# Masked pair products, and transposes and logits moved around one product, in a chunked delta-rule attention with expert routing

## The chip, the cores and the metric

The kernel runs on one core of one Trainium2 chip. The metric is the device time of one execution, in microseconds (us). A core has a matrix engine (TensorE, PE in the profile, with its weight loads listed as PEld), a vector engine (VectorE, DVE), an activation engine (ScalarE, ACT), a general engine (GpSimd, POOL) and a queue that issues transfers (SyncE, SP). Each engine runs its own instructions in order, and waits by semaphores for the others. Matrix products land in PSUM, eight banks of 2 KB per partition, from which ScalarE or VectorE copy them to SBUF.

## The reference

Two blocks follow each other. The first is the delta rule, for 4 batches, 8 heads, 768 steps and a head size of 48; the second sends each of the 3,072 resulting rows of 384 numbers through one of 16 experts, chosen by two argmax steps.

```python
k_n = k / (norm(k) + 1e-6)
for t in range(S):
    y[:, :, t] = q_t @ state
    v_old = state.T @ k_t
    state = state + beta_t * outer(k_t, v_t - v_old)
x = y as (B*S, H*D)
group = argmax(x @ w_group);  expert = argmax(x @ w_expert[group])
out = softmax weight of group * softmax weight of expert * (relu(x @ w1[expert]) @ w2[expert])
```

## The kernel before

**Tiling.** The 768 steps are cut into 24 chunks of 32 (`C = 32`, `NCH = 24`). The 4 batches of a chunk lie on the 128 partitions, 32 steps each (`quads`); `pairs` are the two halves of 64 partitions, two batches each. Four chunks make a group (`RG = 4`); a group's triangular systems, one per chunk, batch and head, are inverted together on VectorE with one system per partition.

**Stages.** `gram(u)` computes the products of keys with keys and of queries with keys of chunk u (L229). ScalarE copies the first to `gt` (L234), which the inverse reads, and, in `rest()`, the second to `raw` (L240); GpSimd multiplies `raw` with the triangular mask `upper` into `gq` (L242). Grams run nine chunks ahead (`LEAD = 9`). `inverse(g)` is VectorE's long task: a transpose of `gt` (L253), the norms, some 90 elimination steps (L304 to L332), and a transpose back into `mt` (L339). `spread(u)` has ScalarE copy `mt` twice into `mtb`, once for even and once for odd batches with zeros in the other (L347), so that one product of 64 rows and 64 columns can serve two batches.

`advance(u)` is the serial part, in five steps:
1. `a`: keys times the state, onto the scaled values in `a_ps` (L367, after VectorE's `scale`, L353); ScalarE copies it, negated, to `f` (L371); `o`: queries times the state into `o_ps` (L376)
2. `w` = inverse times `f` (L384), copied by ScalarE (L387)
3. the state product of keys and `w` into `s_ps` (L394), and ScalarE's copy of the first half of the state to `s_bd` (L401)
4. the copy of the second half
5. the inner outputs, `gq` times `w`, added to `o_ps` (L407), and the copy to `x` (L411)

`logits(u - 1)` has two steps for the chunk before: transposes of `x` (L428), copied to `xt` (L432), and the router's products (L436), copied to `lg` (L438). `route(r)` does the argmax, softmax, ranks (`rk`, L505) and places for a group of chunks on VectorE; its counts are products on TensorE (L499, L500); the sorting products (L540) gather each token's place into `s_sort`, a part of `s_ps`.

**PSUM.** `s_ps` holds four banks, `a_ps` and `o_ps` one each. `g_ps` is one tile of two banks, and is shared: Gram products use both, `w` bank 1, transposes and logits bank 0, the ranks' counts the end of bank 1.

**Order.** The order on each engine is written out by hand. The loop over u, from 0 to 24, calls the steps of `advance` and `logits` in turn, and between them `work(n)` and `allow(...)`. These feed the background tasks (`inverse`, `route`): `work(n)` gives each task n x 180 units times its share, and a task runs steps, each 100 units plus its elements, until its credit is spent. A task that yields a word (`NEXT`, `SOON`, `SORT`, `RANK`, `PE_STEP`, `ACT_STEP`, `TURN`) stands until `allow` is called with that word. `inverse(g)` for the group two ahead starts at the end of the period of the third chunk of a group, at share `SHARE`; the call of `gram` for its last chunk has just gone out. After the loop, the last routings are finished, the tokens' places are read, and the expert stage begins: 16 experts, two tiles of tokens each, nearly all on TensorE.

Of the kernel before, what the change touches and what calls it, by code (L numbers as in the profile page):

```python
# [8 lines left out]
F32 = mybir.dt.float32  # L9
# [5 lines left out]

C = 32
RG = 4
SHARE = 0.9
LEAD = 9
FIXED, TILE = 2, 128  # L20
SLOTS = [224] * FIXED + [232, 220, 214, 208, 204, 202, 200, 196, 192, 188, 184, 182, 176, 168]
# [4 lines left out]
def constants(n_tokens, seq, n_experts, n_group, n_batch):  # L26

    import numpy as np

    p = np.arange(128)  # L30
    i, k = np.meshgrid(np.arange(C), np.arange(C), indexing="ij")
    u = np.arange(n_tokens // 128)

    ids = np.stack([(p[:, None] // C) * seq + p[:, None] % C + u * C - n_tokens,
                    u * 128 + p[:, None]], axis=2)
    out = {
        "upper": np.concatenate([(i < k).astype(np.float32)] * n_batch, axis=0),
        "tiny": np.full((128, 1), 1e-36),
        "eps": np.full((128, 1), 1e-6),
        "parity": np.stack([p // C % 2 == b2 for b2 in range(2)], axis=1),  # L40
        "below": np.tile(-(i > k).astype(np.float32).reshape(1, C * C), (128, 1)),
        "ident": (p[:, None] == p[None, :]),
        "before": (p[:, None] < p[None, :]),
        "ones": np.ones((128, 128)),
        "desc": np.tile(np.arange(n_group, 0, -1), (128, RG)),
        "ids": ids.reshape(128, -1),

        "places": np.tile((2 * np.arange(TILE) + np.arange(2)[:, None]).reshape(1, -1), (128, 1)),


        "tie": np.tile(n_experts - 1 - np.arange(n_experts) + (1 << 20) * (np.arange(n_experts) < FIXED), (128, 1)),
        "slots": np.tile(SLOTS, (128, 1)),
        "expert": np.tile(np.arange(n_experts), (128, 1)),
    }
    at, n = {}, 0
    for name, a in out.items():
        at[name] = (n, n + a.shape[1])
        n += a.shape[1]
    return np.concatenate([a.astype(np.float32) for a in out.values()], axis=1), at
# [3 lines left out]
def deltanet_then_moe(  # L63
# [90 lines left out]
    with ExitStack() as first:  # L154
# [61 lines left out]
        def gram(u, home=None, parts=slice(0, 2)):  # L216


            g, uu = divmod(u, RG)
            kqt = kqt_[u % NB]  # L220
            if uu == 0 and parts.start == 0:
                gts[g] = wk.tile([128, C, RG, H], F32, tag="gt", name=f"gt{g}")
            g_out = (g_ps if home is None else home).rearrange("p f (j x) -> p (f j) x", j=NP)[:, :, 0:2 * C].rearrange(
                "p h (a t) -> p h a t", a=2)
            for j in range(NP):
                for b in range(B):
                    for hh in range(2):
                        rows = slice(hh * 64, hh * 64 + D)
                        nc.tensor.matmul(g_out[quads[b], hh * NP + j, parts],  # L229
                                         lhsT=kqt[rows, 0, j, quads[b]],  # L230
                                         rhs=kqt[rows, parts, j, quads[b]], start=True, stop=True,
                                         skip_group_check=True)
            if parts.start == 0:
                nc.scalar.activation(  # L234
                    gts[g][:, :, uu].rearrange("p t h -> p h t"), g_out[:, :, 0, :],
                    ACT.Copy)

            def rest():
                raw = wk.tile([128, H, C], F32, tag="raw", name=f"raw{u}")
                nc.scalar.activation(raw, g_out[:, :, 1, :], ACT.Copy)  # L240
                gqs[u] = wk.tile([128, H, C], F32, tag="gq", name=f"gq{u}", bufs=LEAD + 1)
                nc.gpsimd.tensor_tensor(  # L242
                    gqs[u], raw, cut["upper"][:, None, :].to_broadcast([128, H, C]), op=ALU.mult)

            return rest

        def inverse(g):

            m = wk.tile([128, C, C], F32, tag="m", name=f"m{g}")
            flat = m.rearrange("p i j -> p (i j)")
            nc.vector.transpose(out=flat, in_=gts.pop(g).rearrange("p t u h -> p (t u h)"))  # L253
# [105 lines left out]
        def advance(u):  # L359

            g, uu = divmod(u, RG)
            kqt = kqt_[u % NB]
            k = kv_[u % NV][:, 0:H * 64].rearrange("p (j d) -> p j d", j=NP)
            if u > 0:
                for j in range(NP):
                    for b in range(B):
                        nc.tensor.matmul(a_ps[quads[b], 2 * j:2 * j + 2, :],  # L367
                                         lhsT=kqt[:, 0, j, quads[b]], rhs=s_bd[:, b, j],
                                         start=False, stop=True, skip_group_check=True)
            f = wk.tile([128, H, D], F32, tag="f", name=f"f{u}")  # L370
            nc.scalar.activation(f, a_ps, ACT.Copy, scale=-1.0)  # L371
            o_ps = ps.tile([128, H, D], F32, tag="o", name=f"o_ps{u}")
            if u > 0:
                for j in range(NP):
                    for b in range(B):
                        nc.tensor.matmul(o_ps[quads[b], 2 * j:2 * j + 2, :],  # L376
                                         lhsT=kqt[:, 1, j, quads[b]], rhs=s_bd[:, b, j],
                                         start=(j == 0), stop=False, skip_group_check=True)
            yield
            mt = mtbs.pop(u)  # L380
            w_ps = g_ps[:, 1, 0:H * D].rearrange("p (h d) -> p h d", h=H)
            for h in range(H):
                for b in pairs:
                    nc.tensor.matmul(w_ps[b, h], lhsT=mt[b, (h % 2) * NP + h // 2],  # L384
                                     rhs=f[b, h], start=True, stop=True, skip_group_check=True)
            w = wk.tile([128, H, D], F32, tag="w", name=f"w{u}")
            nc.scalar.activation(w, w_ps, ACT.Copy)  # L387
            yield


            if u < NCH - 1:
                for j in range(NP):
                    for b in range(B):
                        nc.tensor.matmul(s_at[:, b, j], lhsT=k[quads[b], j],  # L394
                                         rhs=w[quads[b], 2 * j:2 * j + 2],
                                         start=(u == 0 and j == 0), stop=True,
                                         skip_group_check=True)
            for hh in range(2):
                rows = slice(hh * 64, hh * 64 + D)
                if u < NCH - 1:  # L400
                    nc.scalar.activation(s_bd[rows, :, :, hh, :],  # L401
                                         s_at[rows, :, :, hh * D:(hh + 1) * D], ACT.Copy)
                yield
            gq = gqs.pop(u)
            for h in range(H):
                for b in quads:
                    nc.tensor.matmul(o_ps[b, h], lhsT=gq[b, (h % 2) * NP + h // 2], rhs=w[b, h],  # L407
                                     start=(u == 0 and h == 0), stop=True,
                                     skip_group_check=True)
            x = wk.tile([128, DM], F32, tag="x", name=f"x{u}", bufs=4)  # L410
            nc.scalar.activation(x, o_ps.rearrange("p h d -> p (h d)"), ACT.Copy)  # L411
            xs[u] = x
            yield
# [134 lines left out]
        def start(task, share):  # L548
            behind.append(task)
            rate[task], due[task] = share, 0.0  # L550
# [33 lines left out]
        with tc.manual_schedule(engines={mybir.EngineType.PE, mybir.EngineType.DVE,  # L584
# [5 lines left out]
            masks = []  # L590
            for u in range(RG):
                gram(u, homes[u % len(homes)], slice(0, 1))
                if u == 0:
                    nc.tensor.matmul(a_ps.rearrange("p h d -> p (h d)"), lhsT=kqt_[0][:, 0, 0],
                                     rhs=kqt_[0][:, 0, 0:H * D // 128], start=True, stop=True)
                if u == 1:

                    nc.scalar.activation(kqt_[0][:, 1, 0, 0:1], cut["tiny"], ACT.Copy)
                    load_rest()
            start(inverse(0), 1)  # L600
            work(16)
            for i, u in enumerate(range(LEAD)):
# [18 lines left out]
            for u in range(NCH + 1):  # L621
# [12 lines left out]
                allow(ACT_STEP)  # L634
                if u + 1 < NCH and (u + 1) // RG in mts:
                    spread(u + 1)
                work(16)
                next(step)
                next(turned)
                allow(SORT)  # L640
                allow(RANK)
                if u and u + 1 < NCH:
                    scale(u + 1)
                work(9)
                next(step)
                next(turned)
                next(step)
                next(step)
                mask = gram(u + LEAD) if u + LEAD < NCH else lambda: None
                work(8)  # L650
                allow(PE_STEP)
                r = group_of.get(u - 1)
                if r is not None and group_of.get(u) != r and r >= NGR - 2:
# [281 lines left out]
```

## Time and profile before

The median of three runs is 571.86 us (570.44 to 572.13); the profiled execution has a span of 571.6 us.

| engine | busy us | share of the span | instructions |
|---|---|---|---|
| TensorE | 486.6 | 85% | 8376 |
| VectorE | 253.6 | 44% | 889 |
| ScalarE | 178.2 | 31% | 384 |
| GpSimd | 124.6 | 22% | 134 |

The shares mix two stages. The attention stage takes about the first 275 us, and VectorE's work lies nearly all in it; the expert stage takes the rest. A line of the timeline has a start, a duration, the engine, the line of the code, what it wrote and read, the shapes, a count of merged instructions, and in brackets the idle time before it with the instruction that ended it. The shape `64*64 64x48` on TensorE is 64 rows and 64 columns of weights, and 48 columns streamed.

### The profile page before, as it was taken

The numbers are of one execution on the slowest core, as the hardware profiler recorded it, in microseconds if no ns is written. First come the engines' busy times: TensorE is split into PE (matmuls) and PEld (weight loads), VectorE is DVE, ScalarE is ACT, GpSimd is POOL, SyncE is SP. The second block draws the span as 40 slices with busy tenths as digits, with TensorE's granted clock in tenths as the row PEclk, the third lists the DMA queues.
The fourth block names the chain that finished last, engine by engine and source line by source line (L and its number), as shares of the span: only waits on it lengthen the run. The fifth ranks groups of instructions, "written<-read, shape, count | busy, mean of one in ns | idle before, by whom it ended". The sixth has DMA issues, their size and how long they took to land.

```text
span 571.6 us, 18945 instructions
## 1 busy us (share of the span) xinstructions
PE 486.6 (85%) x8376; PEld 459.2 (80%) x8376; DVE 253.6 (44%) x889; ACT 178.2 (31%) x384; POOL 124.6 (22%) x134
## 2 busy tenths in 40 slices
PE   4227778788888887887699999999999999999993
PEld 3226667677787777787599999999999999999992
DVE  3999979799899597323601101011111111111110
ACT  2124436655664555651012111111111111111110
POOL 0130001121222111211432212342215321221111
PEclk9999768989986999997599999999999999999998
DMA  6913535766641123300157656676676775676400
GB/s 192 404 58 89 157 127 170 221 177 188 208 136 52 58 87 95 95 31 16 50 159 205 212 156 222 175 227 208 203 246 155 258 236 190 224 243 226 150 20 20
DMA packets 44900, 90.68 MB, mean 159 GB/s; under 512 B 9819, under 2 KB 29714, under 8 KB 44816
## 3 DMA queue, kind: packets, MB, share of 16 engines
q1 hardware_dynamic: 34832, 79.71, 42.6%
q0 software_dynamic: 9984, 9.74, 6.5%
q8 instruction: 67, 1.10, 0.8%
q14 instruction: 17, 0.14, 0.1%
HBM read 79.92 MB, written 9.66 MB: 157 GB/s over the span
## 4 chain that ended last, share of the span: by engine, by line
issue 33%; PE 21%; DVE 19%; POOL 12%; DMA 9%; ACT 4%; SPq 0%; POOLq 0%; ACTq 0%
DMA out_dram<-yo,to_i 8%; POOL xg L737 7%; POOL out_dram L788 5%; DVE t L326 4%; DVE m L332 4%; PE s_ps L394 3%; PE g_ps L384 3%; DVE m L309 3%; PE o_ps L407 2%; PE a_ps L367 2%; PE g_ps L229 2%; PE g_ps L436 2%; PE g_ps L428 2%; PE s_ps L540 2%; PE o_ps L376 2%
## 5 line engine op out<-in xcount | busy, mean ns | idle before, releaser
L758 PE MATMUL h_ps<-xt,w 128*128 128x224 f32 (+14 forms) x768 | 140.6, 337 | 0.6 <-DVE xt L749 0.6
L772 PE MATMUL y_ps<-hid,w 128*128 128x224 f32 (+14 forms) x768 | 138.8, 334 | 0.0
L758 PEld LDWEIGHTS h_ps<-xt,w 128*128 128x128 f32 x768 | 131.4, 193 | 1.6 <-DVE xt L749 0.9
L772 PEld LDWEIGHTS y_ps<-hid,w 128*128 128x128 f32 x768 | 129.3, 190 | 0.3
L749 DVE COPY xt<-t_ps 128x336 f32<-128x336 f32 (+14 forms) x32 | 15.1, 472 | 141.4 <-PE t_ps L747 141.4
L761 ACT ACTIVATE hid<-h_ps 128x448 f32<-128x448 f32 (+14 forms) x64 | 32.3, 505 | 128.2 <-PE h_ps L758 105.2
L787 DVE TENSOR_SCALAR yo<-o_ps,gate 112x384 f32<-112x384 f32 (+14 forms) x32 | 19.6, 616 | 106.3 <-PE o_ps L784 106.3
L737 POOL DMA_INDIRECT xg<-x_dram,from_i x32 | 39.2, 1224 | 117.1 <-PE t_ps L747 100.6
L788 POOL DMA_INDIRECT out_dram<-yo,to_i x32 | 39.2, 1224 | 101.9 <-DVE yo L787 101.0
L774 ACT ACTIVATE yt<-y_ps 128x224 f32<-128x224 f32 (+14 forms) x48 | 16.2, 338 | 120.2 <-PE y_ps L772 120.2
L326 DVE TENSOR_TENSOR t<-m 128x81 f32<-128x81 f32 (+13 forms) x156 | 53.3, 342 | 0.1
L332 DVE TENSOR_TENSOR m<-m,t 128x81 f32<-128x81 f32 (+13 forms) x156 | 52.3, 336 | 0.0
L242 POOL TENSOR_TENSOR gq<-raw,con 128x256 f32<-128x256 f32 x24 | 20.1, 841 | 135.3 <-ACT raw L240 135.3
L401 ACT ACTIVATE s_bd<-s_ps 48x768 f32<-48x768 f32 x46 | 37.0, 804 | 26.3 <-PE s_ps L394 25.8
L309 DVE SCALAR_TENSOR_TENSOR m<-m 128x29 f32<-128x29 f32 (+27 forms) x174 | 44.0, 256 | 0.4
L384 PE MATMUL g_ps<-f,mtb 64*64 64x48 f32 x768 | 30.6, 230 | 15.7 <-ACT mtb L347 11.2
L384 PEld LDWEIGHTS g_ps<-f,mtb 64*64 64x64 f32 x768 | 27.1, 145 | 20.7 <-ACT mtb L347 11.4
L534 POOL TENSOR_SCALAR at<-con,place 128x256 f32<-128x256 f32 x20 | 20.7, 1040 | 47.0 <-PE s_ps L540 17.2
L394 PE MATMUL s_ps<-w,kv 32*128 32x96 f32 x736 | 29.9, 305 | 0.6 <-ACT w L387 0.6
L229 PE MATMUL g_ps<-kqt 48*32 48x64 f32 (+1 forms) x1280 | 20.5, 253 | 10.3 <-issue 6.5
L428 PE MATMUL g_ps<-con,x 128*128 128x128 f32 x72 | 14.2, 310 | 16.7 <-ACT w L387 16.1
L394 PEld LDWEIGHTS s_ps<-w,kv 32*128 32x128 f32 x736 | 25.9, 210 | 3.1 <-issue 1.5
(118 smaller groups left out, 537.2 us busy)
## 6 DMA issues: line engine op xcount, KB each, us to landing
w<-in_w_dram SPq DMA_DIRECT2D x28, 1536.0 KB, 10.1
kv<-in_kv_dram SPq DMA_DIRECT2D x24, 448.0 KB, 3.3
kqt<-in_kq_dram SPq DMA_DIRECT2D x20, 512.0 KB, 4.5
x_dram<-x SPq DMA_DIRECT2D x24, 192.0 KB, 2.8
w<-in_w_dram SPq DMA_DIRECT2D x6, 512.0 KB, 4.1
w<-in_w_dram SPq DMA_DIRECT2D x4, 576.0 KB, 4.7
kqt<-in_kq_dram SPq DMA_DIRECT2D x8, 256.0 KB, 3.8
w<-in_w_dram SPq DMA_DIRECT2D x2, 384.0 KB, 4.1
```

Source lines behind the costliest of these rows:

```text
L229: nc.tensor.matmul(g_out[quads[b], hh * NP + j, parts], lhsT=kqt[rows, 0, j, quads[b]], rhs=kqt[rows, parts, j, quads[b]], start=True, sto ...
L309: nc.vector.scalar_tensor_tensor(row, in0=m[:, j, 0:j], scalar=m[:, i, j:j + 1], in1=row, op0=ALU.mult, op1=ALU.add)
L326: nc.vector.tensor_tensor(tv, m[:, j + 2:, j:j + 1].to_broadcast([128, n, j]), m[:, j:j + 1, 0:j].to_broadcast([128, n, j]), op=ALU.mult)
L332: nc.vector.tensor_tensor(below, below, tv, op=ALU.add)
L384: nc.tensor.matmul(w_ps[b, h], lhsT=mt[b, (h % 2) * NP + h // 2], rhs=f[b, h], start=True, stop=True, skip_group_check=True)
L394: nc.tensor.matmul(s_at[:, b, j], lhsT=k[quads[b], j], rhs=w[quads[b], 2 * j:2 * j + 2], start=(u == 0 and j == 0), stop=True, skip_group_ ...
L401: nc.scalar.activation(s_bd[rows, :, :, hh, :], s_at[rows, :, :, hh * D:(hh + 1) * D], ACT.Copy)
L737: nc.gpsimd.indirect_dma_start(out=xg[0:P, t, :], out_offset=None, in_=x_dram[:, :], in_offset=bass.IndirectOffsetOnAxis(ap=rows[0:P, t:t ...
L758: nc.tensor.matmul(h_ps[:, k], lhsT=w1[:, j, (f + k) * 128:(f + k + 1) * 128], rhs=xt[:, j], start=(j == 0), stop=(j == DC - 1), skip_grou ...
L761: nc.scalar.activation(hid[:, f:f + 2], h_ps, ACT.Relu)
L772: nc.tensor.matmul(y_ps, lhsT=w2[:, f, j * 128:(j + 1) * 128], rhs=hid[:, f], start=(f == 0), stop=(f == FC - 1))
L788: put = nc.gpsimd.indirect_dma_start(out=out[:, :], out_offset=bass.IndirectOffsetOnAxis(ap=to[0:P, i:i + 1], axis=0), in_=yo[:, :], in_of ...
```

## The change

It has four parts.

- **Inner outputs.** The 32 products of a chunk (8 heads, 4 batches; 32 rows, 32 columns) become 16 (8 heads, 2 pairs; 64 rows, 64 columns). For that, `gq` gets two blocks of 32 columns for each head, one for even and one for odd batches, and the mask `upper` has zeros where a batch's rows meet the other's columns. GpSimd writes 512 elements per partition instead of 256.
- **Transposes and logits.** The transposes of chunk u - 1 go out ahead of `w` of chunk u, right after the copies of `spread`, instead of behind `w`; the logits go out right behind `w`, ahead of the sorting and state products, instead of behind the state products.
- **Inverses and places.** An inverse from the third group on waits for the start of the next period, and `SHARE` falls from 0.9 to 0.85. The ranks' step is allowed near the end of the period instead of in its middle, so the places come a period later.
- **Start.** A product that zeroes `a_ps` goes behind the first four Gram products.

The purpose is fewer and larger products, other work for TensorE around the copies of `w`, and no VectorE instruction that stands in front of a Gram product just issued.

```diff
-SHARE = 0.9
+SHARE = 0.85
...
-        "upper": np.concatenate([(i < k).astype(np.float32)] * n_batch, axis=0),
+        "upper": np.concatenate([(p // C % 2 == b2)[:, None]
+                                 * np.concatenate([i < k] * n_batch, axis=0) for b2 in range(2)],
+                                axis=1),
...
-                gqs[u] = wk.tile([128, H, C], F32, tag="gq", name=f"gq{u}", bufs=LEAD + 1)
+                gqs[u] = wk.tile([128, H, 2, C], F32, tag="gq", name=f"gq{u}", bufs=LEAD + 1)
+                like = [128, H, 2, C]
                 nc.gpsimd.tensor_tensor(
-                    gqs[u], raw, cut["upper"][:, None, :].to_broadcast([128, H, C]), op=ALU.mult)
+                    gqs[u], raw[:, :, None, :].to_broadcast(like),
+                    cut["upper"].rearrange("p (a t) -> p a t", a=2)[:, None].to_broadcast(like),
+                    op=ALU.mult)
...
+            if g > 1:
+                yield NEXT
             m = wk.tile([128, C, C], F32, tag="m", name=f"m{g}")
...
             for h in range(H):
-                for b in quads:
+                for b in pairs:
                     nc.tensor.matmul(o_ps[b, h], lhsT=gq[b, (h % 2) * NP + h // 2], rhs=w[b, h],
...
                 gram(u, homes[u % len(homes)], slice(0, 1))
-                if u == 0:
-                    nc.tensor.matmul(a_ps.rearrange("p h d -> p (h d)"), lhsT=kqt_[0][:, 0, 0],
-                                     rhs=kqt_[0][:, 0, 0:H * D // 128], start=True, stop=True)
                 if u == 1:
...
                     load_rest()
+            nc.tensor.matmul(a_ps.rearrange("p h d -> p (h d)"), lhsT=kqt_[0][:, 0, 0],
+                             rhs=kqt_[0][:, 0, 0:H * D // 128], start=True, stop=True)
...
                     spread(u + 1)
+                next(turned)
                 work(16)
                 next(step)
                 next(turned)
                 allow(SORT)
-                allow(RANK)
                 if u and u + 1 < NCH:
                     scale(u + 1)
                 work(9)
                 next(step)
-                next(turned)
                 next(step)
                 next(step)
                 mask = gram(u + LEAD) if u + LEAD < NCH else lambda: None
                 work(8)
+                allow(RANK)
                 allow(PE_STEP)
```

## The prediction

> **What bounds the kernel now.** I read the page's engine shares and slices first, then the list of waits over the first 275 us, then one chunk in the timeline, and last the groups kept apart by shape.
>
> ```profile
> PE   4227778788888887887699999999999999999993
> DVE  3999979799899597323601101011111111111110
> PEclk9999768989986999997599999999999999999998
> ```
>
> Each digit is a slice of 14.3 us. The expert stage, from slice 20 on, is full of matmuls and the diff doesn't touch it. The attention stage is slices 0 to 19. VectorE looks full there, so the question is whether TensorE waits for it or it for TensorE:
>
> ```profile
> DVE rk L505 <- ACT xt L432: 21.1, 4, 9.6
> PE g_ps L428 <- ACT w L387: 16.1, 22, 3.7
> DVE m L253 <- ACT gt L234: 14.6, 4, 5.9
> PE g_ps L436 <- DVE rk L505: 2.0, 3, 1.0
> PE a_ps L367 <- DVE a_ps L353: 2.0, 2, 1.5
> ```
>
> Columns: who waited, for whom, us in total, times, longest. From 40 to 262 us TensorE names VectorE for 4.0 us, while VectorE stands 35.7 us waiting for copies that follow TensorE. So the loop over chunks is bound by the chain TensorE to ScalarE and back; VectorE runs ahead. The second thing to see is which waits these are. The transposes (L428) write bank 0 of `g_ps` and wait for the copy of `w` out of bank 1; `rk` reads bank 1 and waits for a copy out of bank 0; L436 waits for `rk`. No data pass between these. All accesses to `g_ps` from different engines stand in program order, as one object.
>
> One chunk without a Gram product (u = 20) shows the whole chain:
>
> ```profile
> 232.03 0.87 PE L367 MATMUL a_ps<-s_bd,kqt 128*32 128x96 f32 x32 [0.30 <-ACT s_bd L401]
> 232.71 0.84 PE L376 MATMUL o_ps<-s_bd,kqt 128*32 128x96 f32 x32
> 232.96 0.49 ACT L371 ACTIVATE f<-a_ps 128x384 f32<-128x384 f32 x1 [0.47 <-PE a_ps L367]
> 233.35 0.90 ACT L347 ACTIVATE mtb<-mt,con 128x256 f32<-128x256 f32 x2
> 233.51 1.14 PE L384 MATMUL g_ps<-f,mtb 64*64 64x48 f32 x32
> 235.23 0.55 PE L428 MATMUL g_ps<-con,x 128*128 128x128 f32 x3 [0.59 <-ACT w L387]
> 235.61 0.54 PE L540 MATMUL s_ps<-mine,at 128*128 128x48 f32 x4
> 235.81 0.49 ACT L432 ACTIVATE xt<-g_ps 128x384 f32<-128x384 f32 x1 [0.64 <-PE g_ps L428]
> 236.09 1.15 PE L394 MATMUL s_ps<-w,kv 32*128 32x96 f32 x32
> 237.16 0.85 PE L436 MATMUL g_ps<-wr,xt 128*128 128x20 f32 x6
> 237.94 0.88 PE L407 MATMUL o_ps<-w,gq 32*32 32x48 f32 x64
> 238.26 0.81 ACT L401 ACTIVATE s_bd<-s_ps 48x768 f32<-48x768 f32 x1
> 239.12 0.87 PE L367 MATMUL a_ps<-s_bd,kqt 128*32 128x96 f32 x32 [0.29 <-ACT s_bd L401]
> ```
>
> Start-to-start gives 7.09 us: a to w 1.48, w to transposes 1.72 (0.59 idle), transposes 0.38, sorting 0.48, state to next a 3.03. Today one copy is exposed, that of `w`; the copy `xt` lies beside the sorting and state products.
>
> **What the Trainium skill says.** "PSUM — Partial Sum Buffer", section "PSUM bank collisions raise a hardware error", says to guard by bank and 32-partition quadrant, and that different banks run clean. The trace agrees with a guard but shows a coarser one, over both banks of the tile. "GPSIMD Engine Reference", sections 3.1 and 8, prices a two-input elementwise operation at about 2.6 cycles an element at 1.2 GHz, and says that GpSimd contends with VectorE instructions that have two SBUF inputs. The trace agrees: the mask's 256 elements have a median of 744 ns, and a VectorE operation beside it is held:
>
> ```profile
> 25.40 0.76 POOL L242 TENSOR_TENSOR gq<-raw,con 128x256 f32<-128x256 f32 x1 [5.57 <-ACT raw L240]
> 25.49 0.91 DVE L332 TENSOR_TENSOR m<-m,t 128x216 f32<-128x216 f32 x1
> ...
> 30.50 0.38 DVE L332 TENSOR_TENSOR m<-m,t 128x216 f32<-128x216 f32 x1
> ```
>
> The same shape takes 0.91 us beside the mask and 0.38 alone: 0.53 us lost per mask. "TensorE: Matmul & The Clock Gate", "What's actually happening", says an idle window of about 3.4 us halves the clock. The trace has such stretches (the 32 state products take 2.04 us at 82.31, after a 3.69 us gap, and 1.15 at 92.72), though shorter gaps also precede some.
>
> **Part by part.**
>
> *Inner outputs.* 64 instructions of 32*32 become 32 of 64*64 with 48 columns: exactly the form of L384. Start to start L407 takes 0.81 us in a Gram chunk (140.79 to the Gram products at 141.60), L384 1.08 (1.14 less the last one's tail). So the part costs about 0.27 us of TensorE more a chunk. Half the instructions buy nothing, because four small tiles ran side by side and only two large ones do. Bounds: 0.55 (half of today) to 1.10; I take 1.08. It has no wait behind `w` that it hadn't before, since the state products precede it.
>
> *The mask on GpSimd, 512 elements.* 744 ns is 256 x 2.17 (the skill's 2.6 cycles) plus about 190; 512 give an estimate of 1.3 us. GpSimd has time (22% busy), and gq is needed nine chunks later. But VectorE would lose another 0.53 us per mask. In the loop VectorE has slack; before it there is none: `inverse(0)` runs without a gap from 11.0 to 45.1 us, the first products wait for its `mt` (11.2 us, "ACT mtb L347"), and all nine early masks (17.75 to 37.4 us) fall in it. 9 x 0.53 = +4.8 us. Bounds 0 (no growth of the stall) to 6.
>
> *Transposes ahead of w.* On ScalarE `xt` now stands before the copy of `w`, and behind the two `mtb` copies. w writes `g_ps`, so by the rule read above it waits for `xt`. Chunk without Gram, from a = 0: transposes follow the o products at 1.48, end 2.03; ScalarE is on `mtb` until 2.22 (234.25 - 232.03); `xt` 2.25 to 2.74; w at 2.80 instead of 1.48. Then 1.72 to the logits, which must wait for the copy of `w`.
>
> *Logits ahead of the state products.* They add 0.78 before the state products; the transposes no longer stand there. Sorting 0.48: state starts at 2.80 + 1.72 + 0.78 + 0.48 = 5.78, instead of 4.06. Behind it the next a waits for both s_bd copies: 1.27 to the first, 2 x 0.81, about 2.92 in all instead of 3.03 (the small `lg` copy no longer lies between them). Inner outputs (1.07 + 1.08) fit in it. Period 8.70: **+1.6 us**, for eight chunks (u = 15 to 22): +12.8. Of the 2.0 us that a waited for VectorE there, all is hidden by the longer chain: -2.0.
>
> *Chunks with Gram (u = 1 to 14).* The `raw` copy ends 1.7 us after a (144.38 - 142.69), `mtb` 2.48. Transposes from 1.75, `xt` 2.5 to 2.99, w at 3.05 instead of 1.75, state at 3.05 + 2.98 = 6.03 instead of 4.33 (147.02 - 142.69). State to a: 1.07 + 1.08 + 0.81 for the Gram products plus about 0.2, 3.16 instead of 3.75 (142.69 - 138.94). **+1.1 us** a chunk: 14 x 1.1 = +15.4.
>
> *Inverses a period later, SHARE 0.85.* This removes VectorE's 14.6 us in front of L253. It is worth something once: at 74.98 the wait of 3.45 us stood ahead of the end of `inverse(1)`, whose `mt` held ScalarE and so TensorE for 3.69 us in all, 3.1 more than the usual 0.59. That goes: -3.1. An inverse costs 25,685 units by its yields, so at 45 x 180 x 0.85 = 6,885 a period it needs 3.7 periods (3.5 before) and starts about a quarter period later. It is still due about a period before its first use, so no new wait is counted.
>
> *Ranks at the period's end.* `rk` no longer holds L436: -2.0 (three waits). It waits for the Gram copy `gt` instead; queued behind it on VectorE are inverse steps with slack. At the end, the two last routings interleave on VectorE after the last logits: the ten small steps of 0.15 to 0.25 us of the earlier one now compete with the later one, about +1.5.
>
> *The zeroing product behind the four Grams.* In front of `gt` it was hidden by the load of the constants (ScalarE's first operation ends at 6.45); 0.
>
> Sum: 571.9 + 4.8 + 12.8 - 2.0 + 15.4 - 3.1 - 2.0 + 1.5 = 599.3. Fewer instructions (1,536 of some 11,000 before 275 us) save about 1 us of the issue gaps, and the cold stretch after the 3.69 us gap (82 to 89 us) may go, some 3 us; more idle time per chunk may bring back about 2. I forecast **597 us**.
>
> **Rivals.**
> 1. *w does not wait for `xt`* (banks guarded apart). Then logits fill the copy of `w`, a chunk gains 0.1 to 0.4 us (some 6 in all), and with -3.1 and -3 for the cold stretch against +4.8: about 564. For it: that is what the order seems meant for. Against: three pairs of accesses on different banks that wait today.
> 2. *The cost is partly hidden*: the clock recovers or VectorE's removed stalls matter more than its waits show, half of the 28 us of both kinds of chunk: about 583. For it: Gram chunks average 9.9 us (48.63 to 197.11 for 15), 1.8 above their clean 8.1, so something else already costs time.
> 3. *A colder clock*: TensorE would be idle 2.1 of 8.7 us a chunk (0.75 before w, 0.59 before the logits, 0.77 before a), today 0.9 of 7.1 (0.59 and 0.30). Five more half-clock stretches of 3 us: about 612. Against: 197 to 250 us has a granted clock of 1.00 with regular gaps.
>
> **Chances.** Forecast 0.55, hidden 0.15, colder 0.15, no wait 0.15. Rival 1 is the only one faster. The range 574 to 616 leaves out most of rival 1 and a tail above rival 3. Faster 0.15, same 0.03, slower 0.82.
>
> **What would show it.** Right: L384 waiting for `xt` about 23 times at 0.7 us, L436 for the copy of `w`; L407 with 768 instructions and about 1.1 us a chunk; L242 near 1.3 us; the first w product near 51 us; chunks near 8.7 us after the last Gram; L253 waiting near nothing. Wrong: w starting right after the transposes while `xt` is copied; masks that don't stretch VectorE; chunks of 7 us after the last Gram.

## The result, and the profile after

The changed kernel takes 622.08 us (620.94 to 625.47) against 572.0 us (570.44 to 577.46) for the kernel before: a ratio of 1.0855, with a 95% interval of 1.0778 to 1.0932. It is slower, as forecast, but by twice what was forecast: +50 us, not +25. Ratios and intervals, here and below, compare only the executions within 1.5% of the fastest of their kernel; medians and ranges are of all its executions, which differ by up to about 3%.

The page of the changed kernel, a slice being 15.6 us here:

```profile
PE   5316968889889888888878999999999999999993
DVE  4999999479679299220144101111111111111110
PEclk9999869678666668677757999999999999999998
```

The attention stage has grown to 21 slices. VectorE is less full than before; TensorE is at 8 or 9 tenths, but look at the third row: most slices from 5 to 18 stand at 0.6 to 0.8, where the row of before had 0.9 in most. From the first to the last state products of the loop the mean granted clock is 0.74, against 0.91 before. TensorE's list of waits from 40 to 305 us:

```profile
PE g_ps L392 <- ACT xt L440: 16.7, 22, 4.2
PE g_ps L392 <- ACT mtb L355: 15.3, 1, 15.3
PE g_ps L444 <- ACT w L395: 13.0, 22, 0.6
PE g_ps L507 <- ACT gt L237: 2.1, 3, 0.7
PE a_ps L375 <- ACT s_bd L409: 1.5, 2, 0.7
```

(Lines have moved by 2 to 8: L392 is w, L440 the copy `xt`, L444 the logits, L436 the transposes, L402 the state products, L415 the inner outputs, L507 the counts of the ranks.) Both waits of the forecast are there, 22 times each: w for `xt`, which it doesn't read, and the logits for the copy of `w`, which they don't read. The second line is the start: 15.3 us for the first `mt`, 11.2 before.

One chunk without a Gram product at full clock, in TensorE's timeline:

```profile
236.94 1.15 PE L402 MATMUL s_ps<-w,kv 32*128 32x96 f32 x32
238.02 1.14 PE L415 MATMUL o_ps<-w,gq 64*64 64x48 f32 x32
239.90 0.87 PE L375 MATMUL a_ps<-s_bd,kqt 128*32 128x96 f32 x32 [0.75 <-ACT s_bd L409]
240.59 0.84 PE L384 MATMUL o_ps<-s_bd,kqt 128*32 128x96 f32 x32
241.36 0.55 PE L436 MATMUL g_ps<-con,x 128*128 128x128 f32 x3
242.55 1.14 PE L392 MATMUL g_ps<-f,mtb 64*64 64x48 f32 x32 [0.65 <-ACT xt L440]
244.28 0.84 PE L444 MATMUL g_ps<-wr,xt 128*128 128x20 f32 x6 [0.59 <-ACT w L395]
```

The next state products start at 245.52: 8.58 us, where 8.70 was worked out. But in 17 of the 23 chunks with state products these take more than 1.4 us (in 4 of 23 before). One of them:

```profile
200.14 2.04 PE L402 MATMUL s_ps<-w,kv 32*128 32x96 f32 x32
202.10 1.95 PE L415 MATMUL o_ps<-w,gq 64*64 64x48 f32 x32
203.98 1.18 PE L232 MATMUL g_ps<-kqt 48*32 48x64 f32 x64
205.09 1.51 PE L375 MATMUL a_ps<-s_bd,kqt 128*32 128x96 f32 x32
206.37 1.51 PE L384 MATMUL o_ps<-s_bd,kqt 128*32 128x96 f32 x32
207.81 0.90 PE L436 MATMUL g_ps<-con,x 128*128 128x128 f32 x3
209.29 1.14 PE L392 MATMUL g_ps<-f,mtb 64*64 64x48 f32 x32 [0.58 <-ACT xt L440]
211.02 0.84 PE L444 MATMUL g_ps<-wr,xt 128*128 128x20 f32 x6 [0.59 <-ACT w L395]
```

The next one starts at 212.44, after 12.30 us. The waits are the same; what differs is the speed of everything from the state products to the transposes: 2.04 us instead of 1.15, 1.95 instead of 1.14. Only w and the logits run at full speed. In this chunk the slow clock comes in right behind the stretch of transposes, wait, w, wait, logits, and goes before it comes round again.

The time splits at the first and the last state products of the loop (before 48.63 and 250.49 us, after 52.43 and 298.83), so that 22 intervals lie between, 15 of them with a Gram product. "Clean" is an interval in which the clock is full, sorting products stand and no other wait does (before 8.08 and 7.09 us with and without Gram, after 8.86, from 141.02 to 149.88, and 8.58):

| part | before | after | change | forecast |
|---|---|---|---|---|
| up to the first state products | 48.6 | 52.4 | +3.8 | +4.8 |
| 22 intervals, clean | 15 x 8.08 + 7 x 7.09 = 170.8 | 15 x 8.86 + 7 x 8.58 = 193.0 | +22.1 | +28.2 |
| the rest of the 22 intervals: slow clock, other waits | 201.86 - 170.83 = 31.0 | 246.40 - 192.96 = 53.4 | +22.4 | -9.1 |
| from there to the end | 321.1 | 324.8 | +3.7 | +1.5 |

### The profile page after: what moved, and what is told of

The parts are those of the page before. It is cut to its first block, busy times and chain, and to the rows that moved or that the text cites. A ratio compares the mean times of both kernels' runs of the same rounds, so it can differ in the third digit from the quotient of the medians.

```text
span 623.6 us, 17404 instructions
## 1 busy us (share of the span) xinstructions
PE 534.7 (86%) x7608; PEld 502.3 (81%) x7608; DVE 265.5 (43%) x889; ACT 178.7 (29%) x384; POOL 136.9 (22%) x134
## 4 chain that ended last, share of the span: by engine, by line
issue 29%; PE 28%; DVE 14%; POOL 11%; DMA 9%; ACT 6%; SPq 1%; POOLq 0%; ACTq 0%
DMA out_dram<-yo,to_i 7%; POOL xg L744 6%; POOL out_dram L795 5%; PE s_ps L402 5%; PE o_ps L415 5%; PE g_ps L392 4%; PE a_ps L375 4%; DVE t L334 3%; PE g_ps L444 3%; DVE m L340 3%; DVE m L317 3%; PE s_ps L548 2%; PE o_ps L384 2%; DMA con<-in_const_dram 2%; PE g_ps L232 2%
## 5 line engine op out<-in xcount | busy, mean ns | idle before, releaser
L246 POOL TENSOR_TENSOR gq<-raw,con 128x512 f32<-128x512 f32 x24 | 33.2, 1390 | 165.0 <-ACT raw L243 147.7
L392 PEld LDWEIGHTS g_ps<-f,mtb 64*64 64x64 f32 x768 | 25.8, 141 | 39.0 <-ACT xt L440 23.3
L392 PE MATMUL g_ps<-f,mtb 64*64 64x48 f32 x768 | 29.0, 227 | 32.7 <-ACT xt L440 17.3
L317 DVE SCALAR_TENSOR_TENSOR m<-m 128x29 f32<-128x29 f32 (+27 forms) x174 | 48.4, 281 | 0.4
L415 PE MATMUL o_ps<-w,gq 64*64 64x48 f32 x768 | 41.1, 281 | 0.0
L415 PEld LDWEIGHTS o_ps<-w,gq 64*64 64x64 f32 x768 | 37.5, 195 | 3.5 <-issue 2.9
L402 PE MATMUL s_ps<-w,kv 32*128 32x96 f32 x736 | 39.3, 374 | 0.6 <-ACT w L395 0.6
L402 PEld LDWEIGHTS s_ps<-w,kv 32*128 32x128 f32 x736 | 34.2, 270 | 2.0 <-ACT w L395 0.8
L444 PE MATMUL g_ps<-wr,xt 128*128 128x20 f32 x144 | 22.7, 288 | 14.2 <-ACT w L395 13.6
```

The costliest lines, as they stand in the source:

```text
L317: nc.vector.scalar_tensor_tensor(row, in0=m[:, j, 0:j], scalar=m[:, i, j:j + 1], in1=row, op0=ALU.mult, op1=ALU.add)
L402: nc.tensor.matmul(s_at[:, b, j], lhsT=k[quads[b], j], rhs=w[quads[b], 2 * j:2 * j + 2], start=(u == 0 and j == 0), stop=True, skip_group_ ...
L444: nc.tensor.matmul(l_ps, lhsT=xt[:, j], rhs=wr[:, j], start=(j == 0), stop=(j == DC - 1))
```

## The experiments

Two theories for the third row. A: the two waits around w leave TensorE so quiet that its clock falls. B: the products of 64 rows and columns draw it down. Each kernel below starts from the one named, and ratios are to the kernel before in the same batch of runs. A clock is TensorE's mean granted clock in the profiled execution, where nothing else is said.

**The parts one at a time.** First the order around w alone, from the kernel before:

```diff
                     spread(u + 1)
+                next(turned)
                 work(16)
...
                 next(step)
-                next(turned)
                 next(step)
                 next(step)
                 mask = gram(u + LEAD) if u + LEAD < NCH else lambda: None
```

> Only the transposes and logits are moved around w. Theory A (the two idle stretches of 0.6 us close together, before and behind w, let the clock fall): most of the loss is here, 605 to 620 us, the page's mean clock near that of the changed kernel (0.87). Theory B (the 64-wide products draw the clock down): 585 to 595 us, the cost of the exposed copy alone (1.1 to 1.6 us a chunk), clock 0.94. Theory C (it takes both parts): 585 to 600 us.

615.18 us, ratio 1.0647 (1.0565 to 1.0729), clock 0.893. Most of the loss is in the move of the transposes and logits, with the small products left as they were. B falls as the main cause.

Then the pairs alone: the wider mask and the 64-wide inner products, as in the change's diff.

> Only the inner products on pairs and the wider mask. Theory A: 578 to 585 us: 4 us later start of the first chunk from VectorE held by the mask, and up to 0.27 us a chunk of TensorE, clock 0.94. Theory B: over 595 us with a clock of 0.90 or less. Theory C: as A.

580.34 us, 1.0067 (1.0023 to 1.0112), clock 0.946. The first state products start at 53.64 us instead of 48.63: VectorE is held 5.0 us by nine wider masks, where 4.8 was forecast. TensorE's waits for it:

```profile
PE g_ps L433 <- ACT w L392: 19.4, 22, 6.9
PE g_ps L389 <- ACT mtb L352: 14.0, 1, 14.0
PE g_ps L441 <- DVE rk L510: 5.4, 4, 1.9
```

Here L433 are the transposes and L389 is w. The wait for the first `mt` grows from 11.2 to 14.0 us, and the Gram products ahead of it end 2.2 us later (37.10 instead of 34.93). The longest wait of the transposes, 6.9 us, is the one in which ScalarE's copy of `w` stands behind `mtb` and so behind the second group's `mt`; it was 3.7 before. The masks hold VectorE there too.

The inverses and ranks, SHARE and the zeroing product alone:

```diff
+            if g > 1:
+                yield NEXT
...
-                allow(RANK)
...
                 work(8)
+                allow(RANK)
```

> Only the inverses a period later, SHARE 0.85, the ranks at the period's end and the zeroing product moved. All theories: 563 to 571 us, 3 us from the wait for mt that goes, up to 3 from the cold stretch behind it, 2 from the ranks, 1 to 3 given back at the end.

576.75 us, level with the 576.3 of the kernel before in the same batch. The ratio, 0.9934 (0.9894 to 0.9974), rests on half of its twelve executions, which spread from 568.22 to 587.7, so a gain isn't shown; 563 to 571 us had been expected. The long wait for `mt` is gone here; TensorE's wait for the copy of `w` is 13.6 us in 23 times with none above 0.6.

All parts but the order (the pairs' edit and the last one together):

> The change without its move of transposes and logits: pairs and mask, inverses and ranks later, zeroing product. Theory A: no slow clock (0.93 or more), 572 to 580 us: the mask's 4 us late start and the pairs' products, less the wait for mt. Were the pairs part of the clock's fall: over 590 us.

580.12 us, 1.0094 (1.0069 to 1.0118), clock 0.954. So the order is what costs: with it the change is at 1.0855, without it at 1.0094. The two parts don't quite make up the whole (1.0647 x 1.0094 = 1.0747), and in the loop the clock was 0.81 with the order alone and 0.74 in the changed kernel: whether the pairs deepen the fall once the order is there was not tried apart. The wait for `mt` is back in this kernel: the transposes wait 5.4 us once, with `mtb` waiting 5.29 us for `mt`.

**More work, less time.** If quiet stretches make the clock fall, work in them must bring it back. From the changed kernel:

```diff
+        def keep_warm(n):
+            for _ in range(n):
+                nc.tensor.matmul(s_ps[:, 1, 384:432], lhsT=ident, rhs=con[:, 0:48], start=False,
+                                 stop=True, skip_group_check=True)
...
                 next(turned)
+                keep_warm(2)
                 work(16)
                 next(step)
+                keep_warm(2)
                 next(turned)
```

> The changed kernel with two products that nobody reads (128 by 128 by 48, 0.47 us together) in each of the two idle stretches around w, so that TensorE has 0.94 us more work a chunk and hardly longer a chain. Theory A: the clock comes back to 0.93 or more, chunks near 9 us, 580 to 595 us, faster than the changed kernel with less work. Theory B: 620 us or more, clock unchanged.

599.11 us (587.91 to 603.37), which is 23 us less than the changed kernel with 200 TensorE instructions more (the kernel before took 576.3 in this batch). The profiled execution, at 597.0 us, has a clock of 0.934 against 0.87. Its clock row:

```profile
PEclk9999978997997799996569999999999999999997
```

TensorE's wait of w (L397) for `xt` in it:

```profile
PE g_ps L397 <- ACT xt L445: 7.7, 21, 2.4
```

It falls from 16.7 to 7.7 us, since products now stand in it. The time is just above the expected range, and close to that of the forecast, 597 us, in which the clock had been taken as before. That fits the chain alone at such a clock, though the sizes of the forecast's terms were off, as shown below.

**Where the waits come from.** The tile of two banks is cut into two tiles of one bank, so that a guard on the tile no longer joins w with the transposes. (A bank is one of the two runs of 512 numbers per partition that `g_ps` has in the edit.) Each Gram copy becomes two half copies:

```diff
-        g_ps = ps.tile([128, 2, 512], F32, tag="g", name="g_ps")
+        g_b = [ps.tile([128, 512], F32, tag=f"g{f}", name=f"g{f}_ps") for f in range(2)]
...
-            w_ps = g_ps[:, 1, 0:H * D].rearrange("p (h d) -> p h d", h=H)
+            w_ps = g_b[1][:, 0:H * D].rearrange("p (h d) -> p h d", h=H)
...
-            t_ps = g_ps[:, 0, 0:DM].rearrange("p (j t) -> p j t", j=DC)
+            t_ps = g_b[0][:, 0:DM].rearrange("p (j t) -> p j t", j=DC)
```

On the changed kernel:

> The changed kernel with the shared two-bank tile cut into two tiles of one bank, so that w no longer waits for the copy xt and the logits no longer for the copy of w; each Gram copy becomes two half copies. Theory A1 (the guard on the tile makes the idle time, and the idle time the slow clock): both waits go, a chunk without Gram falls from 8.6 us at full clock to about 7.1, the mean clock comes back to 0.93 or more, 570 to 585 us. Rival A2 (the clock falls for another reason in this order, such as the row of transposes): clock below 0.90, 600 us or more.

575.28 us, 0.9984 (0.9956 to 1.0011), clock 0.951: 47 us of the 50 are gone, by the ratio all, with the order, pairs and ranks of the change as they were. A chunk without Gram:

```profile
228.27 1.15 PE L410 MATMUL s_ps<-w,kv 32*128 32x96 f32 x32
229.34 1.14 PE L423 MATMUL o_ps<-w,gq 64*64 64x48 f32 x32
231.23 0.87 PE L383 MATMUL a_ps<-s_bd,kqt 128*32 128x96 f32 x32 [0.75 <-ACT s_bd L417]
231.91 0.84 PE L392 MATMUL o_ps<-s_bd,kqt 128*32 128x96 f32 x32
232.69 0.55 PE L444 MATMUL g_ps<-con,x 128*128 128x128 f32 x3
233.16 1.13 PE L400 MATMUL g_ps<-f,mtb 64*64 64x48 f32 x32
234.23 0.84 PE L452 MATMUL g_ps<-wr,xt 128*128 128x20 f32 x6
```

Transposes, w (L400) and logits (L452) follow each other without a wait, and the next state products start at 235.47: 7.20 us instead of 8.58. What TensorE waits for now is VectorE's `scale` (12.1 us in nine waits); what makes it late was not followed up.

On the order alone:

> The order around w alone, with the tile cut in two. Theory A1: 560 to 575 us, about 40 us under the order alone, clock 0.93 or more. Rival A2: over 595 us.

571.42 us, 0.9875 (0.9808 to 0.9943), against 1.0647 uncut.

On the kernel before, where the cut lets the transposes and the sorting product run beside the copy of `w`:

> The kernel before with the tile cut in two: the transposes and the sorting product run beside the copy of w instead of behind it. Theory A1: 0.5 us less a chunk and less idle time, 555 to 568 us. If the half copies of the Grams load ScalarE too much, 570 to 576.

566.6 us, 0.9819 (0.976 to 0.9877). A chunk without Gram, from the state products on:

```profile
231.30 1.15 PE L402 MATMUL s_ps<-w,kv 32*128 32x96 f32 x32
232.38 0.84 PE L444 MATMUL g_ps<-wr,xt 128*128 128x20 f32 x6
233.15 0.88 PE L415 MATMUL o_ps<-w,gq 32*32 32x48 f32 x64
234.33 0.87 PE L375 MATMUL a_ps<-s_bd,kqt 128*32 128x96 f32 x32 [0.30 <-ACT s_bd L409]
```

The next ones start at 237.73, after 6.43 us. So even with the cut the order of the change gains nothing: 7.20 us a chunk against 6.43, and 0.9875 against 0.9819, intervals that overlap. Behind the state products the logits run while a has to wait for the copies of the state anyway (3.03 us from the state products to a here, 2.96 without them in the kernel above). Ahead of the state products nothing hides them.

And with the later inverses and ranks as well:

> The kernel before with the tile cut in two and the inverses and ranks later. If the two gains add: 558 to 565 us. If VectorE's removed waits were slack already: 564 to 568, as with the cut alone.

564.32 us, 0.9784 (0.9713 to 0.9854): the fastest of all, better than both kernels. Whether it beats the cut alone is not settled, for the intervals overlap.

Two unread products in the wait behind w, in the kernel before:

> The kernel before with two unread products in the idle stretch behind w. If the clock is what idle time costs there too: a mean clock of 0.96 or more and 560 to 570 us. If the before kernel's slow stretches come from the longer gaps alone (issue, mt): 570 to 576 us, clock unchanged.

578.31 us, 0.9994 (0.9956 to 1.0032), clock 0.939: nothing. The slow stretches of the kernel before don't come from this wait alone.

**Which move makes the clock fall.** Only the transposes ahead of w, the logits left behind the state products:

```diff
                     spread(u + 1)
+                next(turned)
                 work(16)
                 next(step)
-                next(turned)
                 allow(SORT)
```

> From the kernel before, only the transposes go ahead of w; the logits stay behind the state products. The chain: the exposed copy xt costs 0.8 us a chunk at full clock (7.9 us without Gram). Theory A, if the clock falls by the idle time in a chunk: two waits of 0.6 us stay, so the clock falls too, to about 0.90, and 600 to 612 us. If the clock stays at 0.94, the chain alone: 588 to 595 us, and the logits' move made the clock fall.

587.59 us, 1.0225 (1.0152 to 1.0299). The profiled execution is the fastest of the four, at a clock of 0.948; the others have 0.915 to 0.929, against 0.917 to 0.951 for the kernel before. So the loss is mostly the chain's. The expectation counted two waits, and was wrong in part. A chunk with sorting products and one without:

```profile
207.58 0.55 PE L428 MATMUL g_ps<-con,x 128*128 128x128 f32 x3
208.77 1.13 PE L384 MATMUL g_ps<-f,mtb 64*64 64x48 f32 x32 [0.65 <-ACT xt L432]
209.84 0.65 PE L540 MATMUL s_ps<-mine,at 128*128 128x48 f32 x4
210.50 1.15 PE L394 MATMUL s_ps<-w,kv 32*128 32x96 f32 x32
```

```profile
98.59 0.55 PE L428 MATMUL g_ps<-con,x 128*128 128x128 f32 x3
99.72 1.13 PE L384 MATMUL g_ps<-f,mtb 64*64 64x48 f32 x32 [0.58 <-ACT xt L432]
101.44 1.15 PE L394 MATMUL s_ps<-w,kv 32*128 32x96 f32 x32 [0.59 <-ACT w L387]
```

Where there is something to sort, it fills the wait behind w. Where there isn't, both waits stand, and here the products behind them run at full speed all the same (1.15 us at 101.44). That speaks against idle time alone as the cause. What the logits' move adds is thin products: each loads 128 columns of weights to stream 20 columns. Theory L: such products count little for the clock, and next to the waits and the transposes they make one quiet stretch. To tell that from mere length, unread products go into the last kernel, at the place where the change puts the logits; they write another tile than `g_ps`, so they run in the wait behind w. Thin ones:

```diff
+            for j in range(DC):
+                nc.tensor.matmul(s_ps[:, 1, 384:404], lhsT=kqt_[u % NB][:, 0, j], rhs=wr[:, j],
+                                 start=False, stop=True, skip_group_check=True)
```

> From the kernel with the transposes ahead of w (587.6 us, clock 0.948), three unread products of the logits' shape (128 rows and columns of weights, 20 columns streamed) are added where the change put the logits, between the wait behind w and the sorting products: 0.78 us more a chunk, and no more idle time. Theory L (products that stream few columns count little for the clock, so two waits, the transposes and such products make one quiet stretch): the clock falls to 0.90 or less and the time to 610 us or more. If only idle time counts: clock 0.94 or more, 598 to 607 us, the added work alone (22 x 0.8 = 17 us, some of it beside other waits).

Dense ones:

```diff
+            for j in range(6):
+                for b in pairs:
+                    nc.tensor.matmul(s_ps[b, 1, 384:432], lhsT=kqt_[u % NB][b, 0, j % NP, 0:64],
+                                     rhs=kv_[u % NV][b, 384 + j * 48:432 + j * 48], start=False,
+                                     stop=True, skip_group_check=True)
```

> As the run with thin unread products, in the same place and for about the same time, but twelve products of w's shape (64 by 64, 48 columns). Theory L: the clock stays at 0.94 or more, 595 to 605 us, clearly faster than with the thin ones. If only idle time or the chunk's length counts: the same as with the thin ones, within 1%.

Thin: 612.53 us, 1.06 (1.0527 to 1.0673), clock 0.89. Dense: 605.01 us, clock 0.92; its ratio, 1.0358 (1.0231 to 1.0485), rests on two of its four executions, but all four (594.15 to 608.8) lie below all four thin ones (611.71 to 613.58). Their clock rows, thin and then dense:

```profile
PEclk9999669788857768976659999999999999999998
```

```profile
PEclk9999768867598799999859999999999999999998
```

At full clock a chunk without Gram is 7.40 us without unread products, 7.99 with the thin and 8.02 with the dense, so in 22 chunks either adds some 13 us. Against the kernel before in their batch, the transposes' move alone costs 11.9 us, with the thin ones 34.5 and with the dense ones 26.9. The thin ones bring the clock down as the change does, to slices of 0.5 to 0.7 at 11 to 14 and again at 17 to 19, although TensorE has less idle time than without them. With the dense ones it recovers from slice 14 on. So shape matters beyond length; but the dense kernel falls too in its first half, and its clock misses the 0.94 that theory L asked for in three of four executions, so shape isn't all.

Last, only the logits moved ahead, the transposes left behind w:

```diff
                 next(turned)
+                next(turned)
                 allow(SORT)
...
                 next(step)
-                next(turned)
                 next(step)
```

> From the kernel before, only the logits move ahead of the sorting and state products; the transposes stay behind w. Quiet in a row: wait behind w, transposes, wait for xt, logits. Theory L: the clock falls as in the order of the change, 0.90 or less, 605 to 620 us. If it takes the transposes ahead of w: clock 0.94, 588 to 600 us by the chain (about 1.4 us a chunk).

611.3 us (605.98 to 621.63); the ratio, 1.0493 (1.0401 to 1.0585), rests on three of the six. Clock 0.888 in an execution of 614.9 us. The transposes ahead of w aren't needed for the fall; it comes with the logits next to the two waits.

The kernels side by side; the last three columns are of one profiled execution, from the first to the last state products:

| kernel | clock, all executions | loop, us | TensorE not busy, us | clock |
|---|---|---|---|---|
| before | 0.917 to 0.957 | 201.9 | 33.6 | 0.91 |
| transposes ahead of w | 0.915 to 0.948 | 207.8 | 38.0 | 0.92 |
| the same with dense products | 0.912 to 0.947 | 233.6 | 35.2 | 0.85 |
| the same with thin products | 0.890 to 0.898 | 238.0 | 27.9 | 0.78 |
| logits ahead of the sorting | 0.875 to 0.909 | 240.8 | 44.1 | 0.79 |
| both moves | 0.875 to 0.901 | 237.4 | 45.5 | 0.81 |
| changed | 0.870 to 0.886 | 246.4 | 34.2 | 0.74 |

The clock doesn't follow the idle time: it is lower with 27.9 us of it than with 38.0. It is lowest in the kernels that have thin products ahead of the state products, next to one or both of the waits.

## Why the forecast was right in direction and wrong in size

**The step that failed** is the clock's term. The forecast put the whole of the clock at about -1 us: "the cold stretch after the 3.69 us gap (82 to 89 us) may go, some 3 us; more idle time per chunk may bring back about 2." Together with the waits that were to go, the third row of the table came to -9.1 us; it is +22.4. That is a net figure: 8.2 us of gaps without a shown reason and the waits for `scale` and `rk` are gone from it, so the clock's own loss is larger. Rival 3 named a colder clock, but from idle time alone and as five more stretches of 3 us, and it was argued against with "197 to 250 us has a granted clock of 1.00 with regular gaps": that row held for an order in which a wait of 0.6 us stood between dense products. The order alone brings the clock to 0.893. Filling the waits of the changed kernel brings it to 0.934 and cutting the tile to 0.951; with the logits left where they were it is 0.915 to 0.948. The Trainium skill's page "TensorE: Matmul & The Clock Gate", section "What's actually happening", which the forecast leaned on, speaks of an idle window of about 3.4 us. In 15 of the 17 slow chunks here no wait is longer than 0.75 us (the other two stand behind the wait for the first `mt` and one of 4.17 us); the measurement decides: in this kernel short waits with thin products beside them suffice.

**The guard on the tile** was read rightly from the waits of before: w waited for `xt` and the logits for `w`, 22 times each, at 0.62 and 0.59 us. Cutting the tile shows it to be the tile's guard. Rival 1 (no such wait) is what the cut makes true, and then the time is 575 us, not its 564: a chunk without Gram takes 7.20 us, 0.11 more than before, where it counted 0.1 to 0.4 less.

**The chain** was right without Gram (8.70 forecast, 8.58 measured) and too long with Gram: +1.1 us was forecast, 0.78 measured (8.08 to 8.86):

```profile
141.02 1.15 PE L402 MATMUL s_ps<-w,kv 32*128 32x96 f32 x32
143.98 0.87 PE L375 MATMUL a_ps<-s_bd,kqt 128*32 128x96 f32 x32
145.73 0.55 PE L436 MATMUL g_ps<-con,x 128*128 128x128 f32 x3 [0.23 <-ACT raw L243]
146.91 1.13 PE L392 MATMUL g_ps<-f,mtb 64*64 64x48 f32 x32 [0.63 <-ACT xt L440]
149.88 1.45 PE L402 MATMUL s_ps<-w,kv 32*128 32x96 f32 x32
```

From state to a it took 2.96 us instead of 3.16, and w started 1.18 us behind the transposes instead of 1.30; that is the difference. This term of the sum was 28.2 and is 22.1.

**The 64-wide products** have the form of w and its cost: 1.06 us in a Gram chunk at full clock (142.10 to 143.16) against 0.81 for twice as many small ones, as forecast. The starts in the traces show why: the small ones start four at a time, a new four every 0.043 us, the large ones two at a time, a new two every 0.058 us; that is 16 rounds either way. (The forecast's lower bound, 0.55, is half of the large ones' cost, not half of the 0.81 of before.)

**The mask** takes 1.33 us at the median (1.3 forecast), and a VectorE instruction beside it is held for about as long. In the changed kernel:

```profile
22.58 1.26 POOL L246 TENSOR_TENSOR gq<-raw,con 128x512 f32<-128x512 f32 x1 [2.54 <-ACT raw L243]
22.61 1.26 DVE L317 SCALAR_TENSOR_TENSOR m<-m 128x7 f32<-128x7 f32 x1
```

The same step took 0.21 us with no mask beside it (at 21.97 in the trace of before), so one mask costs 1.05 us where the forecast had 0.53 twice. The start is 5.0 us later in the kernel with the pairs alone, 3.8 in the changed one (4.8 forecast).

**The inverses.** The forecast's -3.1 us for the wait behind `mt` is right by itself (no wait above 0.6 with the later inverses alone) and wrong in the whole: w waits 4.17 us at 82.16, since three masks in the loop and those before it hold VectorE and bring `mt` late. "L253 waiting near nothing" was wrong: VectorE waits 23.3 us there, more than before, because TensorE is later. It costs nothing.

**The ranks and the end.** No logits wait for `rk`, as forecast. The end costs 2.7 us from the start of the last inner outputs to the copy of the places (258.67 to 271.63 before, 308.93 to 324.56 after), 1.5 forecast; 20 sorting instructions instead of 16 stand in the last row.

## What to carry to other kernels

A wait in the list of waits between two accesses that share no data can, as here, name a guard on the whole tile; before work is moved into the shadow of a copy, see whether the moved work writes the same tile, and if so cut the tile first. Ask too what hides the work where it stands now: the logits were hidden behind the state products. When an order is changed on TensorE, read the granted clock as a cost of its own: look for waits, transposes and thin products in a row, and try dense products between them. A kernel with less work can be slower than the same kernel with unread products in its gaps, as the changed one was; in the kernel before such products gained nothing.

## What was not expected of the hardware

- The clock fell in chunks with no wait above 0.75 us. With both moves of the order it was 0.875 to 0.901 in four executions; with the transposes' move alone, whose waits are as long, 0.915 to 0.948.
- Two kinds of unread products of about the same length at the same place differ: 612.53 us with 20 streamed columns for 128 columns of weights, 605.01 with 48 for 64. What the clock counts is not settled: products with other numbers of columns were not tried.
- TensorE's idle time that ends with nothing the profile shows ("issue") was 8.2 us in nine gaps from 55 to 250 us before, and none in the changed kernel. Over the like stretch the other kernels with 768 inner instructions instead of 1,536 have 0.2 to 2.5 us, those with 1,536 have 5.3 to 17.2. Fewer instructions are the difference that they share; no run tried it by itself.
